# Two trigonometric visits, sums as TensorE products, and paced loads in a gated linear attention with an MLP behind it

## The chip, the cores and the metric

The kernel runs on one core of a Trainium2 chip. The metric is the device time of one execution in microseconds (us). The five engines of the core run their own instruction streams in order: TensorE (PE) multiplies, VectorE (DVE) and ScalarE (ACT) work elementwise, GpSimd (POOL) fills masks, SyncE (SP) issues all the transfers (DMA). An engine waits for another by semaphores only.

## The reference

```python
mag = np.sqrt(a_re * a_re + a_im * a_im)
scale = np.minimum(mag, 0.999) / (mag + 1e-06)
a_re_n, a_im_n = (a_re * scale, a_im * scale)
for t in range(S):                                   # B, H, S, D = 4, 8, 768, 48
    ar, ai = (a_re_n[:, :, t, :, None], a_im_n[:, :, t, :, None])
    new_re = ar * S_re - ai * S_im
    new_im = ar * S_im + ai * S_re
    S_re, S_im = (new_re + einsum('bhd,bhe->bhde', k[:, :, t], v[:, :, t]), new_im)
    y[:, :, t] = einsum('bhd,bhde->bhe', q[:, :, t], S_re)
x = y.transpose(0, 2, 1, 3).reshape(B * S, H * D)    # 3072 tokens x 384
h = x @ w_in                                         # 384 x 2048, float64 weights
g = np.maximum(h, 0.0) + np.log1p(np.exp(-np.abs(h)))
out = (g @ w_out).astype(np.float32)                 # 2048 x 384
```

## The kernel before

The recurrence is computed in chunks of 128 tokens: 6 groups of 4 batches, 24 chunks. A complex decay has a logarithm of its magnitude and an angle, and both are summed along the tokens. Queries and keys are then scaled by exp(+sum) and exp(-sum) and turned by the cosine and sine of the summed angle, and a chunk is plain linear attention: scores, a mask, tokens from the scores and from the state, and a state that takes up the chunk's keys and values.

`pre` prepares a slice (one chunk in the first group, two chunks in the others): DMA of its data (L528), logarithms and exponentials on ACT (L541 to L556) with products on DVE between them, an arctangent (L619), the prefix sums, and a sine and a cosine (L622, L623) behind a second change of ACT's function table (L986). In the first group the sums are products with a triangular matrix on PE (L587), in the others scans on DVE (L566). The list `PARTS` says which slices of the first group share one part of the program. DVE turns queries and keys with L659 and L661.

`chunk` handles one chunk. SP moves the turned queries and keys from SBUF to SBUF into a layout by heads (L707 and L711, four transfers for a chunk), PE transposes the keys (L726), makes the scores in 32-row tiles (L753), the tokens (L786 from the state, L789 from the masked scores) and the state's increment (L815). Scores, tokens and increments use PE in tiles of 32 columns; the program calls that mode 1, everything else mode 0. DVE applies the mask (L757). The tokens go to the tile `xt` as a rounded part (L798) and a remainder (L799).

`moe` multiplies a group's 512 tokens with the weights in 16 blocks: nine products for `h` (L851), softplus on ACT and DVE (L856 to L871), nine products into the three output banks (L887); in the first group the second weights are used unsplit in three slower products (L884). A block of the first group can start only when all four chunks of `xt` are there. `weights` loads the float64 weights (L389), rebuilds float32 from their words on DVE (L399 to L406) and splits them into a rounded part and a remainder (L413, L416).

Nothing runs in the order in which it is written. Each piece is a `Task` with an engine, a duration, a key and its dependencies, and `Planner.order` writes one fixed order for each engine from the keys and costs in the table `K`. Where PE would be idle between the first sum and the first `o` product, the planner puts fillers there, products with the identity whose result nobody reads (L927). They stand in PE's program and run whether PE would have waited or not.

Of the kernel before, what the change touches and what calls it, by code (L numbers as in the profile page):

```python
# [45 lines left out]
PARTS = [(0, 1, 2, 3), ()]  # L46
TRIB = 5
NAT = {"i": 0, "o": 8}
CSTEP = 0.05
FILL = 0.2233  # L50

# [10 lines left out]
W_LIM = 2.0 ** -15  # L62
W_MAX = 3.3e38
CHK_W = 2 * NSL + NI * B
TB = 2

# [21 lines left out]
class Task:  # L88
    __slots__ = ("eng", "dur", "fn", "key", "idx", "deps", "outs", "bufs", "tab", "nbytes", "left", "ready", "end", "alt", "mode")

    def __init__(self, eng, dur, fn, key, idx, tab, nbytes, mode=0):
        self.mode = mode
        self.eng, self.dur, self.fn, self.key, self.idx, self.tab, self.nbytes = eng, dur, fn, key, idx, tab, nbytes
        self.deps, self.outs, self.bufs, self.end = set(), [], [], 0.0
        self.alt = {}


class Planner:
    WIN = 3.4133
    FREE = 0.2  # L100
    SWITCH = (0.13, 0.095)
# [6 lines left out]
    def __init__(self):  # L108
        self.tasks = []
        self.busy, self.warm = [0.0], [False]  # L110

# [17 lines left out]
    def add(self, eng, dur, fn, key, r=(), w=(), tab=None, nbytes=0, mode=0):  # L129
        t = Task(eng, dur, fn, key, len(self.tasks), tab, nbytes, mode)  # L130
# [17 lines left out]
    def order(self, filler, until, gate):  # L148
# [37 lines left out]
        dma_free = 0.0  # L186
# [6 lines left out]
        while done < n:  # L193
# [20 lines left out]
            for e in engines:  # L214
# [4 lines left out]
                if e == "SP" and dma_free > now + K["backlog"]:  # L219
                    for t in pend[e]:  # L220
                        at = max(t.ready, dma_free - K["backlog"]) if t.ready <= now else t.ready
                        nxt = at if nxt is None else min(nxt, at)
                    continue
# [16 lines left out]
                if best is None and e == "PE" and ends and gate.end and not until.end:  # L240
                    t = Task("PE", FILL, filler, 0, -1, None, 0)
                    free[e] = now + self.array(now, t.dur + (self.SWITCH[0] if mode else 0.0))
# [23 lines left out]
                if e == "PE":  # L266
# [3 lines left out]
                    dur = self.array(now, dur)  # L270
                free[e] = now + dur
                t.end = now + dur
                if e == "SP":
                    dma_free = max(dma_free, now + dur + 0.65) + t.nbytes / 330e3
                    t.end = dma_free + 2.0
# [7 lines left out]
        return out  # L283
# [18 lines left out]
class Prog:  # L302
# [16 lines left out]
    def consts(self):  # L319
# [5 lines left out]
        self.fixed = c.tile([P, 4], F32, tag="fixed", name="fixed")  # L325
# [7 lines left out]
        self.wlim = self.const(3, W_LIM)  # L333
        self.wwords = 2 if self.w_in.tensor.dtype == mybir.dt.int64 else 1
# [6 lines left out]
    def masks(self):  # L341
        nc = self.nc
        G, V = nc.gpsimd, nc.vector
        add = self.plan.add
        tri = self.tri = Buf(self.wpool, f"wo{TRIB}", [P, 2 * NI * WCOL], F32, "tri")
        self.masked = Buf(self.cpool, "masked", [1, 1], F32, "masked")

        def draw():
# [7 lines left out]

        add("POOL", 3.0, draw, -1e5, w=[tri])
        add("DVE", 0.3, lambda: V.tensor_copy(self.mask.rearrange("p z t -> p (z t)"), tri()[:, : 2 * P]),
            -1e5, r=[tri], w=[self.masked])
        FIXED["att"] = [self.ps.tile([P, 512], F32, tag=f"att_{j}", name=f"att{j}", bufs=1) for j in range(NATT)]  # L360
# [4 lines left out]
    def weights(self):  # L365
# [5 lines left out]
        for j in range(2 * NWP):  # L371
# [19 lines left out]
            add("SP", 0.45, load, k - K["rlead"], w=[raw], nbytes=n * self.wwords * 4 * P)  # L391
# [17 lines left out]
            def split(k, bits, fin=fin, n=n):  # L409
                def flat(t, i):  # L410
# [5 lines left out]
                add("DVE", d1(n), lambda: V.tensor_tensor(  # L416
                    flat(fin, 1), bits()[:, :n].bitcast(F32), flat(fin, 0).bitcast(F32), ALU.subtract),
                    k, r=[bits, (fin, 0)], w=[(fin, 1)])
# [47 lines left out]
    def pre(self, si):  # L466
# [60 lines left out]
        for j, w in enumerate((ca, sa)):  # L527
            add("SP", 0.45, lambda j=j: nc.sync.dma_start(  # L528
                region(j), self.dense[:, base + 2 * j * W : base + 2 * (j + 1) * W].rearrange("p (c n) -> p c n", c=m)),
                k + 0.1 * j, w=w, nbytes=8 * W * P)  # L530
        for c in range(m):
# [3 lines left out]
                K["chunk"][gc] - K["vlead"], w=[vt], nbytes=4 * VW * P)  # L535
            if not last:
                vo = self.vo[gc] = Buf(p, "g", [P, GT], F32, f"vo{gc}", NG) if gc in (1, 2, 3) else Buf(p, "vo", [P, VO], F32, f"vo{gc}", 1)
                add("SP", 0.45, lambda vo=vo, gc=gc: nc.sync.dma_start(vo()[:, :VO], self.vpad[:, gc, VW:]),
                    K["state"][gc] - K["vlead"], w=[vo], nbytes=4 * VO * P)
# [12 lines left out]
        add("DVE", d1(W), lambda: V.scalar_tensor_tensor(v1(), re(), 0.5, v1(), ALU.mult, ALU.add),  # L552
            at(), r=ra, w=[t1])
        add("ACT", a1(W, 1), lambda: A.activation(re(), v1(), AF.Exp, bias=self.leps, scale=-1.0),
            at(), r=[t1], w=ra, tab="log")
        add("ACT", a1(W, 1), lambda: A.activation(re(), re(), AF.Ln, bias=self.one), at(), w=ra, tab="log")  # L556
        add("DVE", d1(W), lambda: V.scalar_tensor_tensor(v1(), v1(), LOG_CAP, re(), ALU.min, ALU.subtract),
            at(), r=ra, w=[t1])
# [17 lines left out]
        def sums(j, c, tag, bufs, src, key):  # L576
            ps = Buf(self.ps, tag, [P, 512], F32, f"sum{j}_{si}_{c}", bufs)
            h = NI * CH
            v = lambda: ps()[:, :h]

            def mm():
                if not first:
                    PE.matmul(v(), self.ident, car[j]().rearrange("p (b i) -> p b i", b=2)[:, c, :, None].to_broadcast([P, NI, CH]),
                              start=True, stop=False)
                for i in range(NI):
                    o = i * P
# [724 lines left out]
```

## Time and profile before

| | |
|---|---|
| median of 3 runs | 580.68 us (580.28 to 581.86) |
| the profiled execution | 581.71 us, span of its trace 580.0 us |
| PE, DVE, ACT busy | 95%, 74%, 73% of the span |
| mean granted clock of PE | 0.993 of full |
| first product of the MLP (L851) in the chain | 68.60 us |
| ACT table loads | 1 at the start, 30 in the program |

The time of an execution is 1.71 us longer than the span of its trace, and the profiled one lies 1.03 us above the median. A span is read as three stretches: up to the first `h` product, from there to PE's last product, and the last evacuation and store. The granted clock is given in tenths or hundredths of full speed, 2.4 GHz; the lower level is 1.2 GHz.

### The profile page before, as it was taken

Reading aid. Unit: us, or ns where it says so; the run is one execution under the profiler, and the core shown is the slowest. Engines: PE = TensorE matmul, PEld = TensorE weight load, DVE = VectorE, ACT = ScalarE, POOL = GpSimd, SP = SyncE. Lnnn points to the kernel's source line nnn. Section 1 sums busy time; section 2 is a strip of 40 time slices with the busy share of each in tenths; the row PEclk is TensorE's granted clock in tenths of the full one; section 3 lists DMA queues with packets and bytes.
Section 4 is the critical chain, followed back from the end, with each engine's and each line's share of the span. In section 5 each row is a group of like instructions: output and inputs, shape, how many; then the busy total and the mean of one; then the engine's idle time right before and its main releaser. Section 6 shows DMA issues by size and latency. Waiting matters only on the chain.

```text
span 580.0 us, 14116 instructions
## 1 busy us (share of the span) xinstructions
PE 552.9 (95%) x5952; PEld 441.1 (76%) x5952; DVE 431.5 (74%) x670; ACT 426.0 (73%) x756; POOL 3.8 (1%) x23
## 2 busy tenths in 40 slices
PE   0997899999999999999999999999999999999995
PEld 0997766577577878888888888888878888888874
DVE  6696799999897999988688767776976543454443
ACT  7972496967589799795887857957949899754442
POOL 2000000000000000000000000000000000000000
PEclk9998899999999999999999999999999999999999
DMA  8889910062654414455161433413147976020002
GB/s 321 345 209 309 408 64 0 15 172 82 156 164 99 132 37 111 156 132 173 43 192 47 111 101 95 103 48 110 46 124 235 312 238 211 30 55 0 1 1 57
DMA packets 44275, 76.05 MB, mean 131 GB/s; under 512 B 3760, under 2 KB 29360, under 8 KB 44208
## 3 DMA queue, kind: packets, MB, share of 16 engines
q1 hardware_dynamic: 44208, 75.12, 42.3%
q8 instruction: 47, 0.77, 0.5%
q14 instruction: 20, 0.16, 0.1%
HBM read 51.51 MB, written 4.72 MB: 97 GB/s over the span
## 4 chain that ended last, share of the span: by engine, by line
PE 90%; DMA 3%; ACT 2%; DVE 2%; issue 2%; SPq 1%; ACTq 0%
PE h L851 34%; PE o L887 28%; PE o L884 7%; PE att L753 5%; PE att L786 3%; PE o L927 3%; PE att L789 3%; PE att L815 3%; PE att L726 2%; DMA raw_wo<-w_out_dram 1%; DMA x<-dense_dram 1%; PE y L789 1%; ACT L986 0%; SPq L528 0%; DVE x L617 0%
## 5 line engine op out<-in xcount | busy, mean ns | idle before, releaser
L851 PE MATMUL h<-xt,wi 128*128 128x512 f32 x864 | 220.1, 401 | 1.3 <-DVE lt L867 0.8
L851 PEld LDWEIGHTS h<-xt,wi 128*128 128x128 f32 x864 | 159.7, 188 | 42.2 <-issue 2.9
L887 PE MATMUL o<-gh,wo 128*128 128x512 f32 x480 | 161.5, 397 | 0.0
L867 DVE SCALAR_TENSOR_TENSOR lt<-h,lt 128x512 f32<-128x512 f32 x80 | 54.6, 688 | 94.7 <-ACT lt L858 94.1
L856 ACT ACTIVATE lt<-h 128x512 f32<-128x512 f32 x96 | 56.1, 593 | 69.5 <-PE h L851 64.6
L887 PEld LDWEIGHTS o<-gh,wo 128*128 128x128 f32 x480 | 90.1, 188 | 21.0 <-issue 0.6
L887 PE MATMUL o<-gl,wo 128*128 128x512 f32 x240 | 94.1, 392 | 0.0
L858 ACT ACTIVATE lt<-lt,fixed 128x512 f32<-128x512 f32 x96 | 68.5, 722 | 1.5
L857 ACT ACTIVATE lt<-lt 128x512 f32<-128x512 f32 x96 | 59.9, 632 | 1.6
L871 DVE TENSOR_TENSOR gl<-lt,gh 128x512 fp32r<-128x512 f32 x80 | 54.5, 688 | 4.3 <-PE o L887 1.3
L887 PEld LDWEIGHTS o<-gl,wo 128*128 128x128 f32 x240 | 45.1, 188 | 9.7 <-DVE gl L871 0.2
L884 PE MATMUL o<-gf,raw_wo 128*128 128x512 f32 x96 | 43.5, 594 | 0.0
L986 ACT ACT_TABLE_LOAD x30 | 38.5, 1283 | 0.5
L757 DVE TENSOR_TENSOR a<-att,mask 128x512 f32<-128x512 f32 x48 | 31.4, 684 | 7.6 <-PE att L753 6.5
L566 DVE TENSOR_TENSOR_SCAN t<-hold,t 128x384 f32<-128x384 uint8 x40 | 36.1, 945 | 0.7
L753 PE MATMUL att<-qk 96*32 96x96 f32 (+3 forms) x1536 | 34.2, 237 | 1.8 <-issue 1.8
L753 PEld LDWEIGHTS att<-qk 96*32 96x32 f32 x1536 | 30.5, 111 | 6.2 <-issue 5.4
L884 PEld LDWEIGHTS o<-gf,raw_wo 128*128 128x128 f32 x96 | 17.9, 190 | 17.7 <-issue 16.3
L927 PE MATMUL o<-ident 128*128 128x128 f32 x198 | 28.4, 298 | 0.0
L927 PEld LDWEIGHTS o<-ident 128*128 128x128 f32 x198 | 26.3, 211 | 1.0 <-issue 0.8
L869 DVE TENSOR_SCALAR gh<-lt 128x512 fp32r<-128x512 f32 x52 | 22.0, 425 | 3.6
L870 ACT ACTIVATE gh<-lt 128x512 fp32r<-128x512 f32 x28 | 17.2, 626 | 8.6 <-DVE lt L867 8.6
(97 smaller groups left out, 695.3 us busy)
## 6 DMA issues: line engine op xcount, KB each, us to landing
x<-dense_dram SPq DMA_DIRECT2D x20, 768.0 KB, 5.8
qk<-x SPq DMA_DIRECT2D x48, 288.0 KB, 4.2
raw_wo<-w_out_dram SPq DMA_DIRECT2D x8, 768.0 KB, 8.0
raw_wi<-w_in_dram SPq DMA_DIRECT2D x8, 768.0 KB, 10.5
seen<-w_in_dram SPq DMA_DIRECT2D x16, 384.0 KB, 4.7
seen<-w_out_dram SPq DMA_DIRECT2D x16, 384.0 KB, 4.3
v<-vpad_dram SPq DMA_DIRECT2D x24, 224.0 KB, 2.9
qk<-x SPq DMA_DIRECT2D x48, 96.0 KB, 3.8
```

What stands on the lines that cost most here:

```text
L566: V.tensor_tensor_scan(out()[:, s], self.hold, inc()[:, s], 0.0, ALU.mult, ALU.add)
L753: PE.matmul(psc()[QT * u : QT * (u + 1), hh * P + f : (hh + 1) * P], q[:, h, CH + f : CH + f + QT], q[:, h, f:CH], start=True, stop=True)
L851: PE.matmul(h()[:, :n], w()[:, q, i, fs], xt()[:, x, i], start=k == 0, stop=k == 3 * NI - 1)
L856: add("ACT", a1(n) - 0.04, lambda: A.activation(tv(), h(), AF.Abs), k, r=[h], w=[t])
L857: add("ACT", a1(n), lambda: A.activation(tv(), tv(), AF.Exp, scale=-1.0), k, w=[t], tab="log")
L858: add("ACT", a1(n, 1), lambda: A.activation(tv(), tv(), AF.Ln, bias=self.one), k, w=[t], tab="log")
L867: add("DVE", d1(n), lambda: V.scalar_tensor_tensor(tv(), h(), 0.0, tv(), ALU.max, ALU.add), k, r=[h], w=[t])
L871: add("DVE", d1(n), lambda: V.tensor_tensor(gl(), tv(), gh().bitcast(F32), ALU.subtract), k, r=[t, gh], w=[gl])
L884: PE.matmul(acc[m]()[:, :n], v, gt[0](), start=f == 0, stop=f == NF - 1)
L887: PE.matmul(acc[m]()[:, :n], w()[:, wq, f % 2, ms], x(), start=f == 0 and q == 0, stop=f == NF - 1 and q == 2)
L927: self.nc.tensor.matmul(self.acc0[0]()[:, :P], self.ident, x, start=True, stop=True)
L986: nc.scalar.preload_act_table_set(TABLES[table])
```

## The change

- The first group's slices come in two parts, slices 0 and 1 and then 2 and 3, each with one visit to the trigonometric table for its sines.
- In these slices the magnitude, its cap, both prefix sums, the division by a full turn and the removal of whole turns become PE products into PSUM (`mag`, `sums`, `turn`), read by ACT. Rounding to whole turns is an addition and a subtraction of 1.5 * 2^23. ACT first derives four small matrices from the triangular one.
- The remainder of the first four blocks of `w_in`, and that of the first group's tokens, is a difference formed on PE (L495, L496, L915) and copied out of PSUM.
- The state's increment uses 48 columns for each head in place of 64 and 48.
- From the fifth chunk on, the tokens of an even chunk are put behind the moves of the odd one, and the odd one's scores behind those tokens.
- The planner models waiting of PE for its own instructions, eight transfers in flight and other transfer costs; it drops 30% of each later run of fillers. Loads that would start after 10 us wait for an instruction of another engine that the plan has ended by then (`pace`).
- The table `K` is another one.

The core of the diff; line numbers in the text about the changed kernel are those of the new file:

```diff
-PARTS = [(0, 1, 2, 3), ()]
+PARTS = [(0, 1), (2, 3)]
+KEEP = 0.7
+PACED = 10.0
+    def thin(self, out):
+        runs, run = [], []
...
+        for run in runs:
+            if run[0].start > runs[0][0].start + 2 * self.WIN:
+                drop.update(run[math.ceil(KEEP * len(run)) :])
+        return [t for t in out if t not in drop]
+        def derive():
+            A.activation(part(2), part(0), AF.Copy, scale=-1.0)
+            A.activation(part(3), part(0), AF.Copy, scale=1.0 / TWO_PI)
+            A.activation(part(4), self.ident, AF.Copy, scale=0.5)
+            A.activation(part(5), self.cap.to_broadcast([P, P]), AF.Copy, scale=-1.0)
...
+                    def differ(ps=ps, h=h):
+                        nc.tensor.matmul(ps()[:, : n // 2], self.ident, bits()[:, h].bitcast(F32), start=True, stop=False)
+                        nc.tensor.matmul(ps()[:, : n // 2], self.minus()[:, :P], flat(fin, 0)[:, h], start=False, stop=True)
...
-        add("DVE", d1(W), lambda: V.scalar_tensor_tensor(v1(), re(), 0.5, v1(), ALU.mult, ALU.add),
-            at(), r=ra, w=[t1])
+            def mag():
+                PE.matmul(vl(), self.halfi(), re(), start=True, stop=False)
+                PE.matmul(vl(), self.ident, v1(), start=False, stop=True)
+            add("ACT", a1(W, 1) - 0.05, lambda: A.activation(re(), vl(), AF.Exp, bias=self.leps, scale=-1.0),
+                at(), r=[pl], w=ra, tab="log")
+            add("ACT", a1(W, 1) - 0.05, lambda: A.activation(v1(), vl(), AF.Relu, bias=self.cap, scale=-1.0),
+                at(), r=[pl], w=[t1])
...
             def mm():
+                PE.matmul(v(), self.mcap(), self.minustri()[:, None].to_broadcast([P, NI, CH]), start=True, stop=False)
                 for i in range(NI):
+                    PE.matmul(ps()[:, o], v1()[:, o], self.minustri(), start=False, stop=False)
+                    PE.matmul(ps()[:, o], re()[:, o], self.minustri(), start=False, stop=i == NI - 1)
...
+                        PE.matmul(ab()[:, o], v3()[:, o], self.turntri(), start=i == 0, stop=i == NI - 1)
+                x = add("ACT", a1(W, 1) - 0.05, lambda: A.activation(v5(), va(), AF.Identity, bias=self.magic),
+                        at("turn"), r=[ab], w=[t5])
+                x.alt["DVE"] = (d1(W), lambda: V.tensor_scalar(v5(), va(), MAGIC, None, ALU.add))
+                x = add("DVE", d2(W), lambda: V.tensor_scalar(v5(), v5(), MAGIC, None, ALU.subtract), at("turn"), w=[t5])
+                add("PE", 0.66, lambda: PE.matmul(va(), self.minus()[:, :P].bitcast(F32), v5(), start=False, stop=True,
+                    skip_group_check=True), at("turn"), r=[t5, self.minus], w=[ab], nm=2)
+                x = add("ACT", a1(W) - 0.05, lambda: A.activation(v4(), va(), AF.Abs), at("turn"), r=[ab], w=[t4])
...
+        before = self.flush(moved) if gc > PAIRED and gc % 2 else None
...
+            t = add("PE", 0.585, score, at(), r=[room], w=[psc], mode=1, nm=32)
+            if before:
+                t.deps.add(before)
...
+            if first:
+                add("PE", 0.19, lambda: PE.matmul(y3(), self.minus()[:, :P], hi(), start=False, stop=True, skip_group_check=True), at(), r=[(xt, (gc, 0)), self.minus], w=[y], nm=1)
+                x = add("ACT", a1(DM) - 0.05, lambda: A.activation(lo(), y3(), AF.Copy), at(), r=[y], w=[(xt, (gc, 1))])
...
-                    s = slice(c0, c0 + (D if h % 2 else VP - D))
+                    s = slice(c0, c0 + D)
...
+                elif t.pace and t.start > PACED:
+                    after = max((x for x in done[-60:] if x[0] <= t.start), key=lambda x: x[0])
+                    self.tc.add_manual_dep(ins, after[1].name, mybir.DependencyInfo(
+                        mybir.DependencyClass.Sync, mybir.DependencyReason.DATA), reason="pace")
...
 K = {
-    "mpen": 2.176,
-    "tpen": 0.597,
+    "mpen": 0.121,
+    "tpen": 3.842,
```

What moves on the engines is seen in the order in which each engine's program stands. On ACT before, the stretch of the first group's first visit to the trigonometric table: `x` holds a slice pair's data, `t` a slice's logarithms and angles, `sum` a prefix sum.

```order
L549 ACTIVATE x_110,chk<-t_147 128x384
L551 ACTIVATE x_110<-x_110,fixed 128x384
L986 ACT_TABLE_LOAD
L619 ACTIVATE t_116<-t_116 128x384
L619 ACTIVATE t_122<-t_122 128x384
L619 ACTIVATE t_130<-t_130 128x384
L619 ACTIVATE t_147<-t_147 128x384
L986 ACT_TABLE_LOAD
L607 ACTIVATE x_105<-sum_1_0_171 128x3x128
```

In the changed kernel the same place on ACT; `att` is a PSUM bank that holds the magnitude:

```order
L632 ACTIVATE x_108,chk<-t_135 128x384
L1130 ACT_TABLE_LOAD
L712 ACTIVATE t_130<-t_130 128x384
L712 ACTIVATE t_135<-t_135 128x384
L646 ACTIVATE t_130<-att_94,fixed 128x384
L1130 ACT_TABLE_LOAD
L644 ACTIVATE x_108<-att_94,fixed 128x384
L634 ACTIVATE x_108<-x_108,fixed 128x384
L648 ACTIVATE x_108<-x_108,fixed 128x384
L624 ACTIVATE t_187<-x_155 128x384
```

The first load now stands behind two slices in place of four, and the second pair (`x_155`) begins its logarithms behind the first pair's. Up to the last cosine of the group ACT's program had seven loads and has five.

On PE before, the last chunk of the first group and the first `h` products; `qk` is the layout by heads, `a` the masked scores, `o<-ident` a filler:

```order
L753 MATMUL att_91<-qk_621 32x128
L927 MATMUL o_190<-ident 128x128 x7
L789 MATMUL y_782<-a_0_770,v_405 32x128 x6
L789 MATMUL y_782<-a_1_775,v_405 32x128 x6
L789 MATMUL y_782<-a_0_770,v_405 32x128 x2
L789 MATMUL y_782<-a_1_775,v_405 32x128 x2
L927 MATMUL o_190<-ident 128x128 x7
L851 MATMUL h<-xt_530,wi_629 128x512 x18
```

The same place on PE in the changed kernel:

```order
L862 MATMUL att_94<-qk_551 32x128
L915 MATMUL y_772<-xt_519,minus 128x384
L1069 MATMUL o_211<-ident 128x128 x3
L900 MATMUL y_835<-a_0_826,v_282 32x128 x6
L900 MATMUL y_835<-a_1_829,v_282 32x128 x6
L900 MATMUL y_835<-a_0_826,v_282 32x128 x2
L900 MATMUL y_835<-a_1_829,v_282 32x128 x2
L1069 MATMUL o_211<-ident 128x128 x3
L915 MATMUL y_835<-xt_519,minus 128x384
L1069 MATMUL o_211<-ident 128x128 x3
L992 MATMUL h<-xt_519,wi_642 128x512 x18
```

The seven fillers ahead of each step became three, and a PE product for the remainder of the tokens (L915) came between the last chunk and `h`.

On PE before, a place in the first group's MLP where increments and scores follow one another:

```order
L815 MATMUL att_92<-v_882,kt_1198 32x64 x3
L815 MATMUL att_92<-vo_886,kt_1198 32x48 x3
L753 MATMUL att_91<-qk_1136 32x128
L753 MATMUL att_91<-qk_1136 32x96
L753 MATMUL att_91<-qk_1136 32x64
```

The same stretch of work for the second group's third chunk in the changed kernel, from its last score:

```order
L862 MATMUL att_96<-qk_1458 32x128
L992 MATMUL h<-xt_519,wi_1519 128x512 x9
L897 MATMUL att_94<-qk_1458,s_127 32x128 x16
L900 MATMUL att_94<-a_0_1592,v_1213 32x128 x6
L900 MATMUL att_94<-a_1_1605,v_1213 32x128 x6
L900 MATMUL att_94<-a_0_1592,v_1213 32x128 x2
L900 MATMUL att_94<-a_1_1605,v_1213 32x128 x2
L992 MATMUL h<-xt_519,wi_1519 128x512 x9
```

Ahead of the first `h` PE's program held 92 fillers and holds 42. From the second chunk's scores on, 29 of them stood between the last three chunks; 14 stand there now from the scores of the last chunk but one. The products for the low parts of the weights (16) stand ahead of these scores, and so do, on DVE and ACT, three more rebuilt weight blocks than before and the logarithms of slice 4.

Behind the first `h`, PE's program before goes from mode 0 to mode 1 at 36 places; nine of these visits hold increments and both scores. In the changed program there are 43 such visits, twelve of them with two scores alone.

## Rows read from the trace of the kernel before

**Rows 1.** The page: busy time of the engines, and one transfer queue.
```profile
PE 552.9 (95%) x5952; PEld 441.1 (76%) x5952; DVE 431.5 (74%) x670; ACT 426.0 (73%) x756; POOL 3.8 (1%) x23
...
q8 instruction: 47, 0.77, 0.5%
```
**Rows 2.** Chain that ended last, in order of time: start us, us, what.
```profile
45.93 2.90 issue
...
53.91 1.01 PE y L789 x32
...
56.60 1.76 PE o L927 x14
...
59.85 1.62 issue
...
68.60 4.18 PE h L851 x18
...
567.32 6.23 PE o L887 x27
```
**Rows 3.** Busy us of each engine by stretch, clock, DMA share, GB/s.
```profile
28.00:32.00 4.00, 3.06 (x66) 2.68 (x66) 4.00 (x8) 1.81 (x6) 0.00 (x0) 1.00 0.12 26
...
44.00:48.00 4.00, 1.93 (x48) 1.66 (x46) 3.15 (x5) 0.92 (x4) 0.00 (x0) 1.00 1.02 261
...
64.00:68.00 4.00, 4.00 (x49) 3.49 (x49) 2.01 (x5) 1.07 (x2) 0.00 (x0) 0.70 1.03 400
```
**Rows 4.** ACT in order of time: start us, us, instruction.
```profile
4.38 0.52 ACT L541 ACTIVATE t<-x 128x384 f32<-128x384 f32 x1 [2.28 <-DMA x<-dense_dram]
...
18.87 1.64 ACT L607 ACTIVATE x<-sum 128x384 f32<-128x384 f32 x4
...
25.49 1.28 ACT L986 ACT_TABLE_LOAD   x1
26.79 0.49 ACT L607 ACTIVATE x<-sum 128x384 f32<-128x384 f32 x1
...
39.73 0.60 ACT L623 ACTIVATE t<-t,fixed 128x384 f32<-128x384 f32 x1
```
**Rows 5.** DVE and POOL in order of time, two instructions.
```profile
41.92 0.96 DVE L661 TENSOR_TENSOR x<-x,t 128x768 f32<-128x768 f32 x1
...
2.30 2.64 POOL L354 TENSOR_SCALAR_AFFINE_SELECT tri<-tri 32x128 f32<-32x128 f32 x8
```
**Rows 6.** The moves into `qk`, issued 30 to 34 us, then 45 to 49 us.
```profile
DMA to landing us min/median/max: 3.9/4.2/4.8
...
L711 SPq DMA_DIRECT2D qk<-x x2: 602/602/602, 45.7 to 47.9; - x2
...
DMA to landing us min/median/max: 5.6/6.3/6.8
```
**Rows 7.** The chain inside the first group's MLP: start us, us, what.
```profile
125.36 1.11 PE att L753 x33
126.47 2.29 PE h L851 x9
...
136.30 1.24 PE att L753 x34
...
188.71 2.09 PE h L851 x9
```
**Rows 8.** PE in order of time, pieces of one increment.
```profile
133.05 0.29 PE L815 MATMUL att<-v,kt 128*32 128x64 f32 x6
133.16 0.26 PE L815 MATMUL att<-vo,kt 128*32 128x48 f32 x6
133.24 0.29 PE L815 MATMUL att<-v,kt 128*32 128x64 f32 x6
```
**Rows 9.** PE's waits from 69 to 574 us: total, times, longest.
```profile
PE h L851 <- DVE lt L867: 0.8, 1, 0.8
PE h L851 <- DVE xt L799: 0.6, 1, 0.6
```

More of the change, by code (lines that the diff above doesn't have):

```diff
@@ L110, in __init__, with products @@
         self.busy, self.warm = [0.0], [False]
+        self.issued, self.wanted, self.block, self.dma_free = 0, None, 1, 0.0
+    def products(self, now, dur, nm):
+        size, ask, need, base, most, share, cost = self.FETCH
+        first, self.issued = self.issued, self.issued + nm
+        late = 0.0
+        while True:
+            at = size * self.block + ask - first
+            if self.wanted is None and 0 <= at < nm:
+                t = now + late + dur * at / nm
+                behind = max(0.0, self.dma_free - t)
+                self.wanted = t + base + min(most, share * behind)
+                if behind:
+                    self.dma_free += cost
+            at = size * self.block + need - first
+            if not 0 <= at < nm:
+                return late
+            t = now + late + dur * at / nm
+            late += max(0.0, (self.wanted or 0.0) - t)
+            self.block += 1
+            self.wanted = None
     def array(self, start, dur):
@@ L240, in order @@
                 if best is None and e == "PE" and ends and gate.end and not until.end:
-                    t = Task("PE", FILL, filler, 0, -1, None, 0)
-                    free[e] = now + self.array(now, t.dur + (self.SWITCH[0] if mode else 0.0))
+                    t = Task("PE", FILL, filler, 0, -1, None, 0, 0, 2)
+                    t.start = now
+                    dur = t.dur + (self.SWITCH[0] if mode else 0.0)
+                    late = self.products(now, dur, 2)
+                    free[e] = now + late + self.array(now + late, dur)
                     t.end = free[e]
@@ L611, in pre @@
+            if si == 0:
+                self.gate = opener
+            for k in range(2):
+                add("ACT", a1(W) - 0.05, lambda k=k: A.activation(
+                    cc(k)[:, 0], one(vb()), AF.Exp, scale=-1.0 if k else 1.0), at(), r=[lb], w=ca, tab="log")
+            keep(0, lb, vb, at(), [lb])
         else:
@@ L934, in fast @@
             self.x, self.vt, self.vo = {}, {}, {}
+            self.later = []
             self.opener = None
@@ L987, in fast @@
                 t.fn()
+                ins = nc.cur_bb.bb.instructions[-1]
+                if t.eng in ("ACT", "DVE") or (t.eng == "PE" and t.idx >= 0):
+                    done.append((t.end, ins))
+                elif t.pace and t.start > PACED:
+                    after = max((x for x in done[-60:] if x[0] <= t.start), key=lambda x: x[0])
+                    self.tc.add_manual_dep(ins, after[1].name, mybir.DependencyInfo(
+                        mybir.DependencyClass.Sync, mybir.DependencyReason.DATA), reason="pace")
     def verdict(self, k):
```

297 lines of the change are left out of this document (179 added, 118 removed), and 53 rows, old and new, of the table K.

## The prediction

> **What bounds the kernel now.** First the page's busy line: PE is busy 95% of the span, DVE and ACT some 74% [rows 1]. That is a mean over unlike stretches, so the chain that ended last comes next. Its first `h` product starts at 68.60 us and PE's last one ends at 567.32 + 6.23 = 573.55 us [rows 2]; 6.45 us of evacuation and store follow. Third, PE's waits: between 69 and 574 us there are two, 0.8 and 0.6 us [rows 9]. So 505 us are PE work with 1.4 us of waiting in it, and a change gains there only by taking PE work away. The first 68.6 us are another matter. There PE stood for 2.90 and 1.62 us with no releaser named [rows 2], in a stretch where the transfer engines were fully busy (share 1.02 from 44 to 48 us, with PE busy 1.93 of 4.00) [rows 3], and its program holds 92 filler products ahead of the first `h`. The question is when the first `h` starts and what the 505 us become.
>
> **The change behind the first `h`.** All that the first group needs stands ahead of it in both programs, so the same MLP, 20 chunks of attention and their transposes are left, but for two things.
>
> Visits to mode 1: 36 before, 43 now. Going in costs 0.13 us (two scores take 1.24 us behind an `h`, 1.11 behind an increment), going out 0.20 (an `h` block takes 2.29 us behind a score, 2.09 otherwise) [rows 7]. Seven more visits cost 7 x 0.33 = 2.3 us. Setting an even chunk's tokens before an odd chunk's scores orders the pieces without joining them: most visits hold two scores or one chunk's tokens alone.
>
> The increment: six passes of 64 columns take 0.11 us from start to start, six of 48 columns 0.08 [rows 8]. Four such groups a chunk, 16 chunks: 16 x 4 x 0.03, with 48/64 of 0.11 a little less, 1.8 us saved.
>
> Waits: 1.4 us before. The new program has converted three more weight blocks and done slice 4's logarithms before the first `h`, so DVE and ACT carry less afterwards; but every order is new, and one new wait on DVE of a length like that of the old ones costs 0.6 to 0.8 us. I bound the change of waits by -1.4 and +4 (five or six such), and take 0. The stretch becomes 505.0 + 2.3 - 1.8 = 505.5 us, and the end stays.
>
> **The change ahead of it: the tables and ACT.** ACT's first operation starts at 4.38 us [rows 4], the last turned slice of the first group leaves DVE at 41.92 + 0.96 = 42.88 us [rows 5]. ACT's program up to the last cosine loses two loads of 1.28 us, 2.6 us. It gains: the wait for the triangular matrix, from which ACT now derives four more ahead of its first logarithm (POOL ends at 2.30 + 2.64 = 4.94 [rows 5], 0.6 us later than ACT began); the four derivations, 0.2 us each as an estimate from 0.41 us for three times the columns (1.64 us for four [rows 4]), 0.8 us; four caps, three additions of the magic number, two absolute values and one remainder, ten of 0.41, 4.1 us; one rounding of a weight block with twice the columns, 0.8 us. Two evacuations of keys come behind that point now, 0.4 us each, 0.8 us off. Sum: -2.6 + 0.6 + 0.8 + 4.1 + 0.8 - 0.8 = +2.9 us. The operations that left DVE do not shorten this, since ACT is the longer of the two there. Then ACT waits for PE: magnitude and sums now lie between two ACT operations, for each pair. The trace has no such wait; its bounds are 0 (PE ready when ACT comes) and 3 us (PE at the lower clock), and I take 1.2, under the middle, because the other slice's work fills most of it. The last slice is turned at 42.88 + 2.9 + 1.2 = 47.0 us, between 45.8 and 48.8. Here the change loses: two visits shorten the time to the first pair, not to the last.
>
> A load of 1.28 us at 25.49 us is followed by the next operation at 26.79 us, with no gap [rows 4]. The Trainium skill (ScalarE: Activation LUTs, What ACT_TABLE_LOAD costs) adds a drain of about 1.38 us to each switch, 2.66 us in all. By that two loads fewer would give 5.3 us, and the time below would be 2.7 us lower, 573.7 us; by the row no drain shows, and I stay with 2.6.
>
> **From the last turned slice to the first `h`.** Before, this took 68.60 - 42.88 = 25.7 us. In it lay the moves into `qk`, both gaps of PE, and 29 fillers from the second chunk's scores on, which at 1.76 us for 14 passes of seven products [rows 2] are 58 x 0.126 = 7.3 us, at steps where the mask or the remainder was ready sooner. Now the moves of chunk 2 are issued as one piece: four at 0.6 us each, the last at 47.0 + 1.9 = 48.9 us. They landed 4.2 us after issue at 30 to 34 us and 6.3 us at 45 to 49 us, with loads beside them [rows 6]: 53.1 to 55.2 us; since loads stand ahead of them in the new queue too, I take 54.5. Chunk 3's moves follow 2.4 us behind and are there before PE asks for them. From there PE has two chunks: two times two scores, 2.5 us [rows 7]; two chunks' tokens, 2 x 1.01 us [rows 2]; 14 fillers, 28 x 0.126 = 3.5 us; three remainders at 384/512 of 2.09/9 us, 0.5 us; four ways back to mode 0, 0.8 us. Sum 9.3 us; ACT's rounding and copying of the tokens (0.41 us each) lie under the fillers. The low parts of the weights on PE (16 products) stand ahead of chunk 2's scores, where PE would wait for the moves; without that cover they cost at most 8 x 0.8 = 6.4 us as an estimate by columns from the `h` row, four times as long for plain float32. First `h`: 54.5 + 9.3 = 63.8 us, 4.8 us earlier than before.
>
> The two gaps I count as gone. They fell where the transfer share was 1.02, and instructions come by a queue of their own on the same transfer engines (47 packets [rows 1]); the change lets loads wait. That is inference, since no row names the cause. The Trainium skill (Runtime: NRT & Kernel Launch, Instruction fetch mechanics) holds the refilling of instructions to be mostly hidden; the trace has 2.90 us where nothing else is named. If the page holds, pacing removes nothing, and the rival "the gaps stay" below is the case.
>
> **Sum.** 63.8 + 505.5 + 6.45 = 575.7 us of span against 580.0, 4.3 us less. The profiled execution took 581.71 us, 1.03 over the median; from the median of 580.68 the forecast is 576.4 us.
>
> **Rivals.**
> 1. The way to the first `h` stays as long as before. The weight loads and slice 4 stand ahead of the moves of chunks 2 and 3, landing is late, PE loses its clock while it waits (0.70 from 64 to 68 us [rows 3]) with fewer fillers to hold it, and the 25.7 us recur behind 47.0: first `h` at 72.7, +4.1 + 0.5 = 585.3 us. It decides from a first `h` later than 68.1 us on. For it: the transfer shares of 1.02 and 1.03 [rows 3]; against it: 29 fillers became 14 and the loads wait. Chance 0.14.
> 2. The gaps stay: 4.5 us of PE standing still come back, first `h` at 68.3, 580.9 us. For it: nothing in the trace ties them to the loads but the time. Chance 0.08.
> 3. New waits behind the first `h`: 4 us of them, since the order of everything is new, 580.4 us. For it: the keys of hundreds of tasks changed at once; against it: only 1.4 us before [rows 9]. Chance 0.08.
> 4. A larger gain: ACT never waits for PE (45.8), the moves land in 4.2 us, and the ways back cost nothing beyond the rows (8.5 us): 45.8 + 1.9 + 4.2 + 8.5 = 60.4, 8.2 us earlier, 573.0 us. If the waits of 1.4 us go as well, 571.6. Chance 0.25.
>
> The forecast itself, 573.5 to 578.9 us, has 0.45. What a measurement of this kernel can tell from no change is 0.3%, 578.9 to 582.4 us: that holds rivals 2 and 3, 0.16; faster is the forecast and rival 4, 0.70; slower is rival 1, 0.14. The range from 569 to 584 us leaves out the ends of rivals 1 and 4.
>
> **What would show it.** The table loads on ACT before the first group's last cosine: five. The last turned slice near 47 us; if it is at 43, the ACT sum is wrong. The first `h` near 64 us. No gap of PE over 1 us without a releaser between 40 and 65 us. Behind it, 43 visits at 0.33 us and increments of 0.7 us; from the first `h` to PE's last product 505 to 506 us, and under 503 would mean that the cost of a visit is not what I took. Wrong would be a first `h` after 68 us, or PE's waits over 5 us behind it.

## The result and the profile after

The change made the kernel slower by half a per cent: 583.75 us median of 13 runs (581.78 to 585.99) against 580.76 us of 13 runs of the kernel before (577.78 to 582.37) on the same chip, ratio 1.0052 with a 95% interval of 1.0037 to 1.0068. The forecast was 576.4 us and faster. The time lies inside the range of 569 to 584 us, on the wrong side of no change. One execution of the kernel before among the runs below, 622.59 us at a clock of 0.854, is a slow one and is left out of every figure.

The traces, by the stretches of the forecast; the second trace of before is one of the same kernel, taken for the first experiment below:

| us | before | before, second trace | after | forecast |
|---|---|---|---|---|
| time of the profiled execution | 581.71 | 578.88 | 581.85 | 577.4 |
| span | 580.0 | 577.2 | 579.8 | 575.7 |
| first `h` starts | 68.60 | 65.49 | 65.98 | 63.8 |
| from there to PE's last product | 504.95 | 505.04 | 506.82 | 505.5 |
| evacuation and store | 6.45 | 6.67 | 7.0 | 6.45 |
| mean granted clock | 0.993 | 0.999 | 0.997 | |

Against the second trace of before, the new kernel loses 0.5 us at the first `h`, 1.8 us behind it, 0.3 us at the end and 0.4 us outside the span: 3.0 us. Against the first it gains 2.6 us at the first `h` and loses 1.9, 0.55 and 0.34 us: 0.1 us. The medians differ by 3.0 us; which of the two traces of before is the usual one, experiment 1 asks. The longer end comes back in all traces of the new kernel and is traced to no step.

The page's busy line after, to be laid beside [rows 1]: PE has 6 us more of busy time, DVE and ACT a little less.
```profile
PE 559.1 (96%) x5936; PEld 437.8 (76%) x5936; DVE 430.5 (74%) x675; ACT 422.5 (73%) x754; POOL 5.8 (1%) x30
```
The first half of the forecast's way came true. The last turned slice leaves DVE at 44.83 + 1.82 = 46.65 us (forecast 47.0), where before it was 42.88 [rows 5]; ACT loads five tables ahead of the last cosine. Start us, us, instruction: that end on DVE, and of the five loads on ACT the last two:
```profile
44.83 1.82 DVE L768 TENSOR_TENSOR x<-x,t 128x768 f32<-128x768 f32 x2
```
```profile
26.90 1.28 ACT L1130 ACT_TABLE_LOAD   x1
...
40.22 1.28 ACT L1130 ACT_TABLE_LOAD   x1
```
The gaps of PE without a releaser [rows 2] are gone: between 40 and 66 us no PE wait is put down to "issue", and the clock stays at 1.00. What ends the way to the first `h` now is another thing, and the chain of waits of the kernel after shows it (start us, us, what):
```profile
51.37 2.56 DMA qk<-x
53.94 0.96 DVE x L628
54.90 0.88 DVE t L629
...
55.80 0.97 DVE t L630
...
56.79 0.94 ACT x L632 x2
...
57.76 0.94 ACT x L634
58.69 0.38 ACT xt L916
59.09 1.28 ACT L1130
...
61.25 1.28 ACT L1130
62.54 0.94 ACT x L652
...
63.51 0.94 ACT x L654
64.44 0.39 ACT xt L912
...
64.88 0.44 PE y L915
...
65.98 2.11 PE h L992 x9
...
72.09 2.36 PE h L992 x9
...
566.55 6.25 PE o L1028 x27
```
Lines 628 to 654 are the head of slice 4, the first slice of the *second* group. Its steps, and a trigonometric visit with its two table loads, stand on DVE and ACT between the copies of the tokens of chunks 0, 2 and 3 (lines 911, 912, 916), which the first `h` needs. The copies of chunk 0 and chunk 3 began 1.4 and 1.0 us behind their products (55.3 to 56.67 and 63.3 to 64.35 us), the copy of chunk 0's low part 0.9 us behind its product. In the kernel before, slice 4's first logarithm starts with the first `h` (65.60 us in its second trace).

PE's waits from the first `h` on (us in total, times, longest), beside [rows 9]: 2.4 us instead of 1.4, and the largest is new. `kt` are a chunk's transposed keys, copied out of PSUM; `lt` and `gf` are written by the softplus steps of an `h` block, which the expectations below call softmax.
```profile
PE att L935 <- ACT kt L841: 1.4, 1, 1.4
PE h L992 <- DVE lt L1008: 0.6, 1, 0.6
PE h L992 <- DVE gf L1002: 0.4, 1, 0.4
```

### The profile page after: what moved, and what is told of

The parts are those of the page before. It is cut to its first block, busy times and chain, and to the rows that moved or that the text cites. A ratio compares the mean times of both kernels' runs of the same rounds, so it can differ in the third digit from the quotient of the medians.

```text
span 579.8 us, 14122 instructions
## 1 busy us (share of the span) xinstructions
PE 559.1 (96%) x5936; PEld 437.8 (76%) x5936; DVE 430.5 (74%) x675; ACT 422.5 (73%) x754; POOL 5.8 (1%) x30
## 4 chain that ended last, share of the span: by engine, by line
PE 87%; ACT 6%; DVE 4%; issue 1%; SPq 1%; POOL 0%; DMA 0%; ACTq 0%; POOLq 0%
PE h L992 33%; PE o L1028 28%; PE o L1025 7%; PE att L862 4%; PE att L897 3%; PE att L900 3%; PE att L834 2%; PE att L935 2%; ACT L1130 1%; PE o L1069 1%; DVE x L628 1%; DVE t L629 0%; DVE lt L1008 0%; ACT lt L999 0%; PE sum L682 0%
## 5 line engine op out<-in xcount | busy, mean ns | idle before, releaser
L992 PE MATMUL h<-xt,wi 128*128 128x512 f32 x864 | 219.5, 401 | 1.0 <-DVE lt L1008 0.6
L992 PEld LDWEIGHTS h<-xt,wi 128*128 128x128 f32 x864 | 159.9, 188 | 41.2 <-issue 2.3
L1010 DVE TENSOR_SCALAR gh<-lt 128x512 fp32r<-128x512 f32 x67 | 28.3, 424 | 7.6 <-PE o L1028 4.5
L862 PE MATMUL att<-qk 96*32 96x32 f32 (+3 forms) x1536 | 32.6, 235 | 0.0
L766 DVE TENSOR_TENSOR x<-x,t 128x768 f32<-128x768 f32 x24 | 22.0, 951 | 3.8 <-ACT t L721 3.8
L897 PEld LDWEIGHTS att<-qk,s 96*32 96x32 f32 x640 | 16.2, 109 | 8.1 <-issue 6.6
L768 DVE TENSOR_TENSOR x<-x,t 128x768 f32<-128x768 f32 x24 | 22.2, 951 | 0.0
```

The lines of the kernel that those rows point to most:

```text
L862: PE.matmul(psc()[QT * u : QT * (u + 1), hh * P + f : (hh + 1) * P], q[:, h, CH + f : CH + f + QT], q[:, h, f:CH], start=True, stop=True)
L897: PE.matmul(o(G), s[:, w : w + 32], q[:, h, :CH], start=prim and G < 4, stop=False)
L992: PE.matmul(h()[:, :n], w()[:, q, i, fs], xt()[:, x, i], start=k == 0, stop=k == 3 * NI - 1)
```

## The experiments

**1. Both kernels again, unchanged (b_again, a_again).** What of the two traces is the program, and what the one execution?

> The kernel before once more, for a second trace of it. The first trace holds 4.5 us of gaps with no releaser ahead of the first h (2.90 and 1.62). If these are met or missed by chance, a faster execution (578 to 581 us) shows them shorter and its first h earlier than 68.60 us; if they belong to the program, they return with the same lengths at the same instructions. Ratio 1.000.

> The changed kernel once more, for a second trace of it. The recorded execution took 581.85 us, 1.9 below the median of 583.75. If the executions differ by PE standing still with no releaser, a trace with a time near the median shows such gaps of some 2 us in sum that the first trace lacks; if they differ by the clock of PE, the mean granted clock goes down with the time instead; if by waits on ACT or DVE, the first h product moves from 65.98 us by the same 2 us. Time 582 to 586 us.

Before: 578.55 us median of 10 runs. The chain of its second trace:
```profile
46.05 0.98 issue
...
51.73 2.03 issue
...
58.33 1.62 issue
...
65.49 4.19 PE h L851 x18
...
564.30 6.23 PE o L887 x27
```
The gaps stand at the same three places of the program and sum to 4.63 us; in the first trace it was 4.68 (2.90 and 1.62 [rows 2], and 0.16 at 55.12 us). But the first `h` comes 3.1 us sooner, because PE kept its clock: the same fillers, scores and tokens between the gaps took 3.2 us longer in the first trace, where the granted clock was 0.50 from 50 to 52 us and from 64 to 66 us. The first trace, in stretches of 2 us (busy us of PE, PEld, DVE, ACT, POOL, clock, DMA share, GB/s):
```profile
50.00:52.00 2.00, 2.00 (x38) 1.82 (x31) 1.45 (x3) 0.54 (x1) 0.00 (x0) 0.50 1.03 253
...
64.00:66.00 2.00, 2.00 (x22) 1.73 (x25) 1.45 (x3) 0.00 (x0) 0.00 (x0) 0.50 1.00 398
```
And the second:
```profile
50.00:52.00 2.00, 1.73 (x41) 1.34 (x40) 1.61 (x3) 0.41 (x1) 0.00 (x0) 1.00 1.04 226
```
So 65.5 us is what the program takes at full clock. The usual execution does not have it: of the 105 executions of the kernel before in these experiments, 72 have a mean clock of 0.995 or less, the median is 0.994, and only five reach the 0.999 of the second trace. The first trace, at 0.993, is the more usual kind.

After: 583.68 us median of 6 runs, ratio 1.0062 (1.0029 to 1.0094), first `h` at 66.01 us as before, but 508.35 us from there on instead of 506.8. The difference lies in one place. PE in order of time in the first trace of after (start us, us, instruction, the wait ahead of it):
```profile
269.08 0.29 PE L935 MATMUL att<-v,kt 128*32 128x48 f32 x6 [1.43 <-ACT kt L841]
...
270.55 2.36 PE L992 MATMUL h<-xt,wi 128*128 128x512 f32 x9 [0.58 <-DVE lt L1008]
```
and in the second, with its clock by stretch (busy us of PE, PEld, DVE, ACT, POOL, clock, DMA share, GB/s):
```profile
270.55 3.83 PE L992 MATMUL h<-xt,wi 128*128 128x512 f32 x9 [0.58 <-DVE lt L1008]
```
```profile
270.00:273.00 3.00, 2.45 (x6) 1.96 (x7) 2.64 (x5) 2.55 (x4) 0.00 (x0) 0.57 0.86 218
```
The same nine products take 3.83 us instead of 2.36: behind the two waits PE was granted the lower level, 1.2 GHz, in this execution and not in the other. The two waits take 2.0 us in both traces, and 1.5 us more went with the clock in one of them.

**2. Without pacing (a_nopace).**
```diff
-PACED = 10.0
+PACED = 1.0e9
```


> The changed kernel without the added waits of the loads (the order of all engines is the same). Theory that the loads' share of the transfer engines makes PE stand still: gaps of 1.5 to 4.5 us come back between 40 and 66 us and the time rises by as much. Rival that the waits of the loads hold back slice 4's data, which ACT works on between the last two chunks: the load of slice 4 lands earlier, the first h comes up to 2 us earlier and the time falls by 1 to 2 us. If pacing does nothing: the same within 0.3%.

582.94 us, ratio 1.0053 (1.0024 to 1.0082); first `h` at 65.99 us, and no gap without a releaser. The loads that pacing had held back now come earlier (DMA share 0.97 to 1.04 from 56 to 64 us), and no gap returns. Pacing is not what removed them.

**3. With all fillers (a_keep).**
```diff
-KEEP = 0.7
+KEEP = 1.0
```


> The changed kernel with all planned fillers (16 bursts keep the third that was dropped, 14 more products of 0.25 us, 3.5 us of PE time ahead of the third h). If fillers lie on the way to the first h, the time rises by 1 to 3 us. If ACT's work on slice 4 sets the first h, the fillers before it are hidden, and only the three more behind the second h block show, 0.3 to 0.7 us. If PE's clock suffers from too few fillers in a typical execution, the time falls.

584.04 us, ratio 1.0076 (1.0047 to 1.0104), first `h` at 66.91 us. Thinning the fillers gains 0.9 us at the first `h`; it is not what makes the new kernel slower.

**4. Slice 4 out of the way (a_early).** The planner's list is kept, and single tasks are set behind others (with whatever depends on them), here the head of slice 4 behind the copies, and x<-t and slice 5's logarithms behind the first softplus steps:
```diff
-for t in self.plan.order(...):
+for t in resort(self.plan.order(...), LATER):
+LATER = [(169, 196), (170, 124), (171, 124), (182, 124), (172, 200), (223, 200),
+         (173, 220), (174, 1005), (177, 1010), (178, 1010), (233, 1005), (175, 1006)]
```


> The changed kernel with one thing moved: slice 4's head (the first slice of the second group) no longer stands between the token copies of chunks 0, 2 and 3 on ACT and DVE, nor its x<-t and x_5's logarithms in front of the first softmax steps; same instructions, same loads. Theory A (ACT and DVE reach the copies late because slice 4's work with its two table loads stands in front of them, which is why the first h came at 65.98 and not at 63.8): the copies of y0 and y3 follow their products within 0.3 us instead of 1.4, 0.9 and 1.1 us, the first h comes at 64.4 (63.9 to 64.8), the third h block at 69.5 to 70.2 instead of 72.09, and the time is about 3 us below the changed kernel's: 580.7. Rival B (chunk 3's moves and its scores set the first h): it stays at 65.5 to 66.0 and the time at 583.5. Rival C (slice 4, now some 4 us late, is missed behind the first h): the first h comes at 64.4, but the transposes of chunk 4 at 83.6 wait, and the time is 582.5 to 583.5.

The added code shifts the line numbers by 41: L1033 here is L992 of the changed kernel. The chain's reading was right: the first `h` starts at 63.76 us in PE's timeline, where the kernel after has 65.74 (there a product starts 0.24 us earlier than in the chain, since it overlaps the one ahead), and the third block at 69.51 instead of 72.09. Yet the time is 586.51 us (ratio 1.0105, 1.0084 to 1.0126). PE in order of time:
```profile
63.76 4.43 PE L1033 MATMUL h<-xt,wi 128*128 128x512 f32 x18
...
69.51 2.33 PE L1033 MATMUL h<-xt,wi 128*128 128x512 f32 x9
...
77.38 4.45 PE L1033 MATMUL h<-xt,wi 128*128 128x512 f32 x18 [2.96 <-DVE gf L1043]
```
A wait of 2.96 us, of my own making, swallows the gain: the second gf stood on DVE behind steps of slices 4 and 5 that were late now. The profiled execution, at a clock of 0.998, took 582.48; the four others, at 0.988 to 0.993, 586.3 to 587.5. That is rival C in its sense, at another place than I had named.

**5. The same, with that wait taken away (a_early2).**
```diff
+LATER += [(235, 1011), (236, 1011), (237, 1011), (179, 1016)]
```


> As a_early (first h at 63.99, third h block at 69.51, then a wait of 2.96 us of PE at 74.4 for the second gf, which stood on DVE behind the x<-x and t<-x,t of the next slices), with the second and third gf put in front of those three DVE steps. Theory A (the gain at the first h is real and a_early lost it again in that one wait, and in the lower clock behind it in most executions): no PE wait over 1 us between 64 and 85, the 18 h products that started at 76.66 in the changed kernel start at 74.3 to 75.2, the time is 581.3 (580.5 to 582), 2 to 2.5 us under the changed kernel's. Rival (whatever comes earlier is waited for later, since ACT and DVE are the bound of the first 100 us): a wait of about the same size shows up elsewhere before 130, time 583 to 584.

582.17 us median of 10 runs, ratio 1.0046 (1.0011 to 1.0082); no wait over 0.4 us up to 90 us. The median lies just above the 580.5 to 582 expected, and its ratio to before is not told from the changed kernel's 1.0052. The trace shows the gain: of the 2.0 us at the first `h`, 1.5 are left at the `h` block that started at 87.09 us in the kernel after:
```profile
76.73 2.36 PE L1033 MATMUL h<-xt,wi 128*128 128x512 f32 x9 [0.23 <-DVE gf L1043]
...
85.55 4.46 PE L1033 MATMUL h<-xt,wi 128*128 128x512 f32 x18 [0.32 <-DVE gf L1043]
```
**6. And the wait at 269 us (a_best, a_best_again, a_third).** The softplus steps in hand go in front of the copies of kt on ACT, and chunk 12's increments beside its scores.
```diff
+LATER += [(514, 1287), (516, 1287), (1293, 1287), (495, 1287), (496, 1290),
+          (532, 519), (497, 1295), (498, 1295)]
```


> a_early2 and one more local reordering at 261 to 275 us, where the changed kernel's PE waited 1.4 us for ACT's copies of kt and 0.6 us for DVE: the softmax steps of the h products in hand now stand in front of the copies and of the next slice's steps on ACT, and chunk 12's increments stand beside its scores on PE (one mode visit less). Theory A (those two waits, and the 1.5 us of lower clock that followed them in the repetition's trace, are part of what the change costs): the two waits shrink to under 0.9 us together, time 1 to 2.5 us under a_early2: 579.5 (578.5 to 581). Rival (PE has no other work there: the waits move behind it, to the next gh or to the scores): no change against a_early2.

580.57 us, ratio 1.0001 (0.9969 to 1.0033). PE's waits behind the first `h`:
```profile
PE att L938 <- DVE a L907: 0.9, 1, 0.9
PE h L1033 <- DVE lt L1049: 0.8, 1, 0.8
PE h L1033 <- DVE gf L1043: 0.5, 2, 0.3
```
The wait for kt is gone, but a wait for masks stands 9 us further on, and the one for `lt` grew: the waits behind the first `h` went from 2.6 to 2.2 us, where the expectation had the two at 269 us fall below 0.9, and the span fell by the same 0.4 us (578.4 to 578.0). By the trace the rival is right. The median is 1.6 us below a_early2's on the same chip, which 10 runs each do not set clear of nothing. So the changed kernel and this one were run once more on one chip, 12 runs each.

> The changed kernel once more, unchanged, beside a_best on one chip. Theory A (the changed kernel loses to the kernel before by the late first h, by the waits near 269 us and by the lower clock that follows them in most executions): time 583 to 584, clock 0.993 to 0.997; in the trace the first h at 66.0, the wait for kt at 269 of 1.4 us, and, if the clock falls, it falls behind that wait. Rival (its lower clock comes from somewhere else): the clock falls at another place of the trace, or the same time at full clock.

> a_best once more, unchanged, on the same chip as a_third. Theory A: 2.5 to 3.5 us under a_third, 580 to 581, clock 0.996 or more in most executions, level with the kernel before (ratio 0.998 to 1.002). Rival (the first 10 runs of a_best were lucky draws): under 1.5 us below a_third.

583.02 us (ratio to before 1.0044, 1.0020 to 1.0068) against 580.43 us (1.0009, 0.9985 to 1.0033): 2.6 us for two dozen tasks set in another place, with the same instructions and loads. The changed kernel's span was 580.0 with the kt wait of 1.4 us at the same place and no fall of the clock in that trace. Only two of its 12 executions have a mean clock as low as the 0.994 of a_again's trace, and one at 0.999 took 583.55 us: that the clock falls behind the waits in most executions is not borne out.

The reordered kernel is level with the kernel before and does not beat it. It is level by its clock: the median of the mean clocks is 0.998, against 0.996 for the changed kernel and 0.994 for the one before (22, 31 and 105 executions on several chips). At one and the same mean clock the medians of the changed kernel lie 3.7 to 4.6 us above those of the kernel before (at 0.994, 0.996 and 0.997: 584.2, 582.9 and 582.9 against 580.2, 579.2 and 578.3), those of the reordered one 1.1 to 2.4 us (at 0.996, 0.997 and 0.998: 580.3, 580.8 and 580.3 against 579.2, 578.3 and 578.1). So the new order costs more than the medians show, and a clock that is kept better hides a part. That the missing gaps keep the clock is likely: from 40 to 66 us it stays at 1.00 in the traces of the changed kernel, and it falls behind a gap in four of five traces of the kernel before and its variants below. No run tries it alone.

**7. What the gaps of the kernel before hang on (b_late, b_late2, b_late3).** Here loads are held back in the kernel *before*: each waits for the last token copy of chunk 3 (task 183) or chunk 2 (164); in b_late slice 4's first step on ACT is also set behind the first softplus steps.
```diff
+PACE = {186: 183, 187: 183, 829: 183, 212: 183, 859: 183}    # b_late
+PACE = {829: 183, 212: 183, 859: 183}                        # b_late2
+PACE = {186: 164, 187: 164, 829: 183, 212: 183, 859: 183}    # b_late3
```


> The kernel before with five loads (slice 4's two, one of slice 5, two of W_in) held back until chunk 3's last token copy, and slice 4's first steps on ACT put behind the first softmax steps; nothing else. Theory A (the PE gaps without a releaser, 0.98, 2.03 and 1.62 us in the second trace of before, come when the 16 DMA engines are full, 1.01 to 1.08 of their time between 40 and 66 us): the DMA share falls under 0.8 behind 53 us, the third gap (1.62) goes and the second (2.03) shrinks or goes, the first stays; first h at 61.9 to 63.9 instead of 65.5; time 577 to 579. Rival B (the gaps belong to places of the instruction stream, whatever the queues carry): all three stay within 0.5 us, first h at 65.5, time 580.5 to 581.5. Rival C (the loads are missed later): gaps go, but PE waits behind the first h by as much.

> The kernel before with only three loads (two of W_in, one of slice 5) held back until chunk 3's last token copy; slice 4's loads stay where they were. Theory A (gaps of PE without a releaser come under a full DMA queue): DMA share under 0.9 from 57 us on, the third gap (1.62 us) goes, the first two stay (their stretch is full of the moves of chunks 2 and 3); no new wait behind the first h; first h at 63.9, time 579 (578 to 580). Rival B (the gap moves with the instruction stream): three gaps, first h 65.5, time 580.7. Rival C (the weights of W_in are late then): a wait over 1 us at 70 to 80, time 581 or more.

> The kernel before with slice 4's two loads held back until chunk 2's last token copy and two loads of W_in and one of slice 5 until chunk 3's; the order on the other engines is that of before. In b_late, where the DMA engines were idle from 56 to 64 us, the third gap was gone; in b_late2, where they stayed full until 58 us, it stood at 1.62 us. Theory A (a gap comes where the DMA engines are full some microseconds ahead of it): here they are nearly empty from about 53 to 57 us, the third gap is under 0.3 us, the first two sum to 1 to 3 us as before; slice 4's first logarithm on ACT waits for its load by up to 1 us; first h at 61.5 to 63.9, time 578.5 (577.5 to 579.5). Rival B (the gap at chunk 3's scores belongs to its place in the stream and was absent in b_late by chance): 1.62 us again, first h 65.3, time 580.5. Rival C (slice 4's load is missed): gap gone, but the wait for gf behind the first h takes it back, time 580.5.

Times: 586.45 us (1.0102, 1.0066 to 1.0139), 581.19 (1.0014, 0.9981 to 1.0046), 579.27 (0.9988, 0.9963 to 1.0013). The third gap answers the question. The chain of b_late2, where slice 4's loads still fill the DMA engines from 56 to 58 us:
```profile
45.99 0.65 issue
...
51.34 0.66 issue
...
56.57 1.62 issue
```
```profile
56.00:58.00 2.00, 0.57 (x26) 0.31 (x19) 0.84 (x2) 1.22 (x2) 0.00 (x0) 1.00 1.00 395
```
In b_late and b_late3 the engines are empty there, and the third gap is gone; b_late3's second is gone as well:
```profile
46.52 3.72 issue
```
```profile
50.00:56.00 6.00, 5.75 (x89) 5.58 (x90) 3.59 (x5) 1.27 (x2) 0.00 (x0) 0.50 0.81 229
56.00:64.00 8.00, 8.00 (x221) 7.54 (x220) 5.67 (x10) 1.83 (x3) 0.00 (x0) 0.95 0.06 13
```
Theory A holds for the third gap, in five traces with and without the loads. The first, in a stretch full of the moves of chunk 2 and 3 (share 1.03 to 1.06 from 46 to 48 us), is a lottery: 0.65, 0.98, 1.79, 2.90 and 3.72 us in five traces, and behind the longest the clock was 0.50 for 6 us. The second (0.16, 2.03, 0.98, 0.66 us and none) is not settled: 0.16 us stood under a share of 1.02, and 0.98 in b_late, where the share was 0.90 and then 0.33.

The first `h` did not come as early as expected: 64.64 us in b_late's timeline of PE (65.25 in the second trace of before), and in the chain 65.31 in b_late2 and 67.28 in b_late3, where the longer first gap and the clock took more than the third gap had cost. b_late lost far more behind it: its second softplus step (gf) stood on DVE behind slice 4's first steps, which waited for their load until 73.96 us:
```profile
77.91 2.93 PE L926 MATMUL o<-gf,raw_wo 128*128 128x512 f32 x3 [4.44 <-DVE gf L903]
```
b_late3's median is 1.0 us below that of before, which its interval cannot tell from nothing.

## Why the prediction was wrong

Forecast and measurement differ by 7.35 us; the terms are 2.2 (first `h`), 1.3 (behind it), 0.55 (end), 0.34 (outside the span) and 2.93 (from the profiled execution to the median).

**The failed step: "ACT's rounding and copying of the tokens lie under the fillers."** From chunk 2's scores on, the prediction counted PE's work alone, 9.3 us from 54.5. The scores came at 55.3 us, 0.8 us late, but the first `h` 10.7 us behind them, 1.4 more than counted, since the copies stood behind slice 4's head and its table loads. With slice 4 out of the way (a_early, a_early2) the same way took 8.7 us, and the first `h` came at the forecast place within 0.2 us: 2.0 us are shown to be slice 4. The prediction had named slice 4 in rival 1 as a matter of transfers only, and had even booked its early logarithms as a gain for later; it did not ask which engine would do them ahead of the first `h`. "Slower" had a chance of 0.14 for a first `h` later than 68.1 us; it came with a first `h` at 65.98, so not as rival 1 has it. This step alone does not turn the sign; the terms below were needed too.

**"4.8 us earlier than before" held a gain that no term names.** The 25.7 us and the 68.60 held 3.1 us of lowered clock, which the window at 0.70 [rows 3] showed and the prediction read as a danger of the new kernel only, while it priced the new way at full clock. The new kernel did keep its clock there, and 2.6 of the 4.8 us came. Against the 65.49 of full clock the forecast 63.8 would have been a gain of 1.7 us.

**The tables and ACT: right.** 46.65 for 47.0, five loads; two visits shorten the time to the first pair, not to the last. The sum hides two small errors: ACT's last cosine ends 3.3 us later than before (43.61 us against 40.33 [rows 4]) where 4.1 were counted, with 1.3 us of waits for sums on PE where 1.2 were taken, and another 0.5 us came on DVE, which stands last on the way there and not ACT. The operation behind the load at 59.09 us starts 1.29 us later, at 60.38; the drain that the Trainium skill adds (ScalarE: Activation LUTs, What ACT_TABLE_LOAD costs) shows in no trace here.

**The two gaps: gone, as counted, but not for the reason given.** That they belong to full transfer engines is shown for the third. That pacing would remove them is refuted by a_nopace. Which other part of the new order did is open: full transfer engines do not suffice, since a_nopace has them from 56 to 64 us (0.97 to 1.04) and the kernel after from 40 to 48 us (0.92 to 1.02), and neither has a gap.

**Behind the first `h`: +0.9 for +0.5, and waits of +1.0 for 0.** 505.0 became 506.8, of which 1.0 are waits; the rest, 0.9 us, is what seven more visits and the narrower increments come to, forecast 2.3 - 1.8 = 0.5. No run tries the two terms apart, but the traces tell them apart: from the first piece of an increment to its last, the 16 chunks take 11.5 us in PE's timeline before and 9.7 after, 1.8 us less, as forecast; the rest of the stretch, with the visits in it, grew by some 2.6 us for 2.3. The 1.0 us of waits lies inside the bounds (-1.4 to +4), but the price of one wait was taken from 0.6 and 0.8 us where the new one is 1.4, and without the clock that may fall behind it. Rival 3 is this mechanism; of its 4 us, 1.0 came.

**From the trace to the median: the largest term, and the least explained.** The prediction set the new kernel's median 1.03 us below a profiled execution, as before's was. The trace of before was somewhat late (clock 0.993, median of its kind 0.994), and that of after an early one (581.85, second of 13; clock 0.997, median 0.996), so the sign turned. A step of 0.001 in the mean clock of a span of 580 us is 0.6 us as an estimate, so the clock would explain some 1.2 of the 2.93 us. a_again shows 1.5 us in one execution as lower clock behind the waits at 269 us; but two of the 13, at 0.998, took 584.28 and 584.42 us. The rest varies from run to run and is not settled.

The loss, then, beside the second trace of before: the change took 4.6 us of gaps out of the way to the first `h`, and paid 3.65 us for the later last slice (43.00 to 46.65 us) and 2.0 us for slice 4, and 1.8 us behind the first `h`. The three on the way sum to +1.0 where +0.5 was measured; 15 fewer fillers and later moves lie on that way too and were not measured apart. Moving the tasks back by hand returned 2.6 us.

## What to carry to other kernels

Where a plan pulls work of the next stage ahead, read each engine's order between the steps of the current stage: in-order engines make an early start of the next stage a late end of this one, though every engine looks idle enough on the page. Before subtracting from a point of one trace, check the granted clock of the stretch ahead of it, take a second trace where it is below 1, and lay the mean clock of the traced execution beside those of the other runs. A wait of 2 us in a dense stretch costs more than itself where the clock falls behind it, which it did in one of seven traces here, so waits are to be priced with that chance in them.

## What the runs showed of the hardware

PE stood without a releaser for 0.65 to 3.72 us at one and the same instruction of the kernel before, in a stretch where the DMA engines were full (share 1.03 to 1.06), and for 1.62 us, three times to the hundredth, at another (both traces of before and b_late2, and not where the engines were empty). The Trainium skill (Runtime: NRT & Kernel Launch, Instruction fetch mechanics) holds the refilling of instructions to be mostly hidden; if these gaps are such refills, which no row names, they were hidden in the kernel after and 4.6 us in the open in the kernel before.

Whether the clock falls behind a stand of PE differs from execution to execution of one program. It fell behind 3.72 us (0.50 from 50 to 56 us), 2.90 and 1.79 us (0.50 from 50 to 52 us), and behind 1.62 us in the first trace of before (0.50 from 64 to 66 us) and in b_late2 (0.50 from 60 to 62 us); it did not behind 2.03 and 1.62 us in the second trace of before, nor behind 2.96 us in that of a_early, whose four other executions have means of 0.988 to 0.993. Behind 1.43 + 0.58 us near 269 us it fell in one of the seven traces that hold it.
